# A spectral filter and an MLP on one core: the 24-point Fourier stages on parts of the TensorE array, the filter held in fp32, and results in pairs of PSUM banks

## The chip, the cores and the metric

The kernel runs on one core of a Trainium2 chip. The metric is the device time of one execution in microseconds (us); lower is better. The core has five engines that run side by side, each working through its own instructions in order: TensorE (PE, matrix multiplication; its weight loads are listed as PEld), VectorE (DVE), ScalarE (ACT), GpSimd (POOL) and SyncE (SP). TensorE writes its results into PSUM, a memory of eight banks, each of which holds 512 fp32 values in each of 128 partitions. VectorE or ScalarE must read a result out before its bank can be used again. POOL and SP start most of the transfers (DMA). An engine that has to wait holds back everything that stands behind in its own order.

## The reference

```python
def _attn_ref(x, filt_r, filt_i):                 # x: 8 x 3072 x 256
    X = np.fft.rfft(x, axis=1)
    F = (filt_r + 1j * filt_i)[None, :, :]        # 1537 x 256
    Y = X * F
    return np.fft.irfft(Y, n=x.shape[1], axis=1).astype(np.float32)

def _moe_ref(x, w1, w2, w_out):                   # x: 24576 x 256, w1, w2: 256 x 1024
    h1 = x @ w1
    h2 = x @ w2
    g = np.maximum(h1, h2)
    return (g @ w_out).astype(np.float32)         # w_out: 1024 x 256

def reference(**kwargs):
    ...
    attn_out = _attn_ref(**attn_kwargs)
    B, S, D = attn_out.shape
    x = attn_out.reshape(B * S, D)
    return _moe_ref(x=x, **moe_kwargs)
```

Each of eight sequences is Fourier-transformed along its 3072 positions, multiplied by a filter for each frequency and channel, and transformed back. The result goes, position by position, through two products with a maximum between them, and a third product.

## The kernel before

A transform of 3072 points is done in two stages, since 3072 is 128 x 24. For each batch b there are these pieces:

- **load_x** (POOL's queue): x in six parts, cast to bf16, with 128 positions on the partitions and 24 x 256 values behind them.
- **f1**: the 128-point stage, a matmul with C1 (pa, 512 columns), copied to `at` by ScalarE and written by SP's queue to `ad` in DRAM. **f1_read** reads it back as `bt` in another order, so that the 24 points (real and imaginary) lie on partitions.
- **gen_f2**: sixteen groups g of two frequencies each. A matmul with U (px, 96 x 256 per frequency) is the 24-point stage (called s2 in what follows). VectorE multiplies px by the real and imaginary filter at once into pq (line 384: 1024 results per partition). Two matmuls, with VP and VQ, are the way back (pz, called s3); ScalarE copies pz to `zt`, which SP writes to `zd`. **z_read** fetches `zr` from it in two halves.
- **s4**: for a tile of 512 positions, eight matmuls with G1 (128 columns each) are the 128-point stage back. They go in two halves `dc` of four into a bank each; ScalarE copies the first half and VectorE the second, into y.
- **moe_h(tt, j)** and **moe_o(tt, j)**: the MLP on tile tt in eight steps j. Since max(a, b) = b + relu(a - b), moe_h multiplies y by Wd (w1 - w2) into ph (two matmuls of 512 columns), and a relu makes g. moe_o multiplies y by M (w2 times w_out) and g by Wo into po, and VectorE copies po to `ot`, which POOL's queue writes out.

All results of TensorE but po share six single banks (`ps`); po has two. The instructions of each engine stand in the order in which the program names them (manual_schedule). A main loop runs over 48 tiles, six to a batch, eight steps each, so 48 steps to a batch. In each step come moe_h(tt, j), then moe_o(tt - 1, j), then the pieces that a table `todo` has for this step (load_x, f1 and f2 of later batches), and behind j = 4 mostly s4 of the next tile. Steps are written by hand, such as

```python
plan_f2(b, list(range(0, 34, 2)), 19, 36)
plan_f1(b, b + 2, range(1, 25, 2), 28)
plan_x(b, b + 3, range(5, 48, 4))
```

for b from 3. Before the loop stands the setup: tables of sines (table_c, tables_u, tables_pe), the filter F in bf16 on 96 partitions (loaded in parts, spread by the matmuls of copy_f and by DMA), batch 0's f1 and f2, the MLP's weights, and a few matmuls without use (spin) that keep TensorE going. In batch 0's f2 four of the sixteen products are POOL's.

Of the kernel before, what the change touches and what calls it, by code (L numbers as in the profile page):

```python
# [13 lines left out]
B = 8  # L14
# [3 lines left out]
N1 = 128  # L18
N2 = 24
T = 32  # L20
QP = 96
J = 12
TWO_PI = 6.283184
RND = 12582912.0


@with_exitstack
def kernel(
# [10 lines left out]

    nc = tc.nc
    V, S, G, TE = nc.vector, nc.scalar, nc.gpsimd, nc.tensor

    const = ctx.enter_context(tc.tile_pool(name="const", bufs=1))
    C1 = const.tile([128, 128], BF16)
    G1 = const.tile([128, 128], BF16)
    U = const.tile([QP, T, 2, 48], BF16)  # L60
    VP = const.tile([QP, T, QP], BF16)
    VQ = const.tile([QP, T, QP], BF16)
    F = const.tile([QP, 2, T, D], BF16)
    Wd = const.tile([128, 2, HID], BF16)
    Wo = const.tile([128, 8, D], BF16)
    M = const.tile([128, 2, D], BF16)
    I128 = const.tile([128, 128], BF16)
# [3 lines left out]
    apool = ctx.enter_context(tc.tile_pool(name="apool", bufs=6))  # L71
    bpool = ctx.enter_context(tc.tile_pool(name="bpool", bufs=2))
    pqpool = ctx.enter_context(tc.tile_pool(name="pqpool", bufs=4))
    zpool = ctx.enter_context(tc.tile_pool(name="zpool", bufs=3))
    ps = ctx.enter_context(tc.tile_pool(name="ps", bufs=6, space=bass.MemoryType.PSUM))
    pso = ctx.enter_context(tc.tile_pool(name="pso", bufs=2, space=bass.MemoryType.PSUM))
    zrpool = ctx.enter_context(tc.tile_pool(name="zrpool", bufs=2))
    setup = ExitStack()
    init = setup.enter_context(tc.tile_pool(name="init", bufs=1))
    ctx.enter_context(tc.manual_schedule())  # L80

# [8 lines left out]


    def fsrc(f, row0, dm, nm, dt, nt):
        return bass.AP(f.tensor, f.offset + row0 * D, [[dm * D, nm], [dt * D, nt], [1, D]])

    def load_f(t0, t1):
        for ri, f in enumerate((filt_r, filt_i)):
            for dr in range(2):
                row0, dt = (t0, 1) if dr == 0 else (64 - t0, -1)
                G.dma_start(out=F[24 * dr:24 * dr + 24, ri, t0:t1], in_=fsrc(f, row0, 64, 24, dt, t1 - t0))


    def copy_f(t0, t1, ri, engine):
        for t in range(t0, t1, 2):
            n = min(2, t1 - t)
            pf = ps.tile([QP, 2, D], FP32, tag="ps", name="pf")
            TE.matmul(pf[:, 0:n], DM, F[0:48, ri, t:t + n], start=True, stop=True)  # L106
            if engine is V:
                V.tensor_copy(F[:, ri, t:t + n], pf[:, 0:n])
            else:
                S.activation(F[:, ri, t:t + n], pf[:, 0:n], AF.Copy)  # L110


    F0 = init.tile([QP, 2, D], FP32)

    def load_f0():
        for ri, f in enumerate((filt_r, filt_i)):
            for dr in range(2):
                src = bass.AP(f.tensor, f.offset + 32 * dr * D, [[128 * D, J], [(96 - 64 * dr) * D, 2], [1, D]])
                nc.sync.dma_start(out=F0[24 * dr:24 * dr + 24, ri], in_=src)

    def copy_f0():
        nc.sync.dma_start(out=F0[49:96], in_=F0[1:48])
        nc.sync.dma_start(out=F0[48:49, 1], in_=filt_i[1536:1537, :])
        nc.sync.dma_start(out=F0[48:49, 0], in_=filt_r[1536:1537, :])

    DM = init.tile([48, QP], BF16)
    SW = init.tile([QP, QP], BF16)
    e0 = init.tile([QP, 2], FP32)
    zero = init.tile([128, 1], FP32)
    V.memset(zero, 0.0)  # L130
    pid = init.tile([128, 1], FP32)
    G.iota(pid, pattern=[[1, 1]], base=0, channel_multiplier=1,
           allow_small_or_imprecise_dtypes=True)
    kc = init.tile([128, 2, 2, T], FP32)
    G.iota(kc[:, :, 0], pattern=[[0, 2], [1, T]], base=0, channel_multiplier=0,
           allow_small_or_imprecise_dtypes=True)
    G.iota(kc[:, :, 1], pattern=[[0, 2], [-1, T]], base=64, channel_multiplier=0,
           allow_small_or_imprecise_dtypes=True)
    for c in range(6):
        load_x(0, c)  # L140
    tt_ = init.tile([QP, T], FP32)
    G.iota(tt_, pattern=[[1, T]], base=0, channel_multiplier=0, allow_small_or_imprecise_dtypes=True)

    kb = init.tile([QP, 2, J, 2], FP32)
    k0 = init.tile([QP, 2, J, 2], FP32)
    G.iota(kb, pattern=[[64, 2], [128, J], [64, 2]], base=0, channel_multiplier=0,
           allow_small_or_imprecise_dtypes=True)
    G.iota(k0[:, 0], pattern=[[128, J], [96, 2]], base=0, channel_multiplier=0,
           allow_small_or_imprecise_dtypes=True)
    G.iota(k0[:, 1], pattern=[[128, J], [32, 2]], base=32, channel_multiplier=0,  # L150
           allow_small_or_imprecise_dtypes=True)
    V.memset(DM, 0.0)
    V.memset(I128, 0.0)
    V.memset(SW, 0.0)
    for b0 in (0, 48):
        G.affine_select(out=DM, in_=DM, pattern=[[-1, QP]], compare_op=OP.not_equal,
                        fill=1.0, base=b0, channel_multiplier=1)
    G.affine_select(out=I128, in_=I128, pattern=[[-1, 128]], compare_op=OP.not_equal,
# [99 lines left out]
    def tables_pe():  # L258
# [9 lines left out]
        for t in list(range(2, T, 5)) + [0]:  # L268
# [7 lines left out]
            if len(todo) > 2:  # L276
                swap(*todo.pop(0))
# [314 lines left out]
```

## Time and profile before

| | us |
|---|---|
| three runs | 592.22, 586.09, 596.46 |
| median | 592.22 |
| span of the profiled execution | 584.8 |
| TensorE busy, matmuls | 543.8 (93%) |
| TensorE busy, weight loads | 399.7 (68%) |
| VectorE busy | 327.6 (56%) |
| ScalarE busy | 338.8 (58%) |
| POOL busy | 77.2 (13%) |
| mean granted TensorE clock | 0.970 |

The profiled execution's own time is not on its page beside the span; the fastest of the runs is 1.3 us longer than that span. A matmul's busy time holds its way through the array, which overlaps with the next matmul. So the time that one costs in a row of them is the distance between their starts. The costliest groups are po's matmuls (line 443, 231.3 us), relu on ScalarE (line 423, 177.1) and the products with the filter (line 384, 150.9). The first output leaves at 89.6 us, the last at 580.5.

### The profile page before, as it was taken

To read this page: it belongs to the slowest core of one execution; us is meant where nothing else is said; L and a number is where in the kernel's file an instruction comes from. 1 tells how busy PE (TensorE), PEld (TensorE's weight loads), DVE (VectorE), ACT (ScalarE), POOL (GpSimd) and SP (SyncE) were. 2 spreads that over 40 slices of the span, in tenths; PEclk is the share of its full clock that TensorE was granted. 3 is DMA by queue.
4 is the path that set the end of the run, shared out by engine and by line. 5 is a ranking of instruction groups with operands and counts; after the bars stand their busy time and mean duration, and the time that the engine had idled before them with its cause. 6 is when DMAs were issued, how large, how long until landed. Compare 5 with 4: busy or idle time off the path is not lost.

```text
span 584.8 us, 9932 instructions
## 1 busy us (share of the span) xinstructions
PE 543.8 (93%) x3981; PEld 399.7 (68%) x4050; DVE 327.6 (56%) x423; ACT 338.8 (58%) x608; POOL 77.2 (13%) x131
## 2 busy tenths in 40 slices
PE   4687797999999999997999999999999999999996
PEld 0456554776678667775777777776777777777774
DVE  8845132773368437753567466654765477734342
ACT  5744383565766766763676566655675455554541
POOL 6034510110020011111110002000000000000000
PEclk9985898899999999999999999999999999999999
DMA  8987588575397778989477946894457524241112
GB/s 165 218 149 228 132 195 180 131 180 157 138 229 161 199 211 183 228 203 239 133 174 204 214 115 166 199 215 127 131 155 176 154 100 118 93 124 73 73 59 86
DMA packets 76642, 93.81 MB, mean 160 GB/s; under 512 B 4627, under 2 KB 56389, under 8 KB 75524
## 3 DMA queue, kind: packets, MB, share of 16 engines
q1 hardware_dynamic: 59492, 53.37, 35.7%
q0 software_dynamic: 17104, 39.81, 27.4%
q8 instruction: 31, 0.51, 0.3%
q14 instruction: 15, 0.12, 0.1%
HBM read 56.63 MB, written 50.33 MB: 183 GB/s over the span
## 4 chain that ended last, share of the span: by engine, by line
PE 44%; issue 33%; DMA 16%; POOL 3%; DVE 2%; ACT 1%; POOLq 0%; SPq 0%; DVEq 0%; ACTq 0%
PE po L443 14%; PE ph L418 12%; DMA bt<-ad 6%; PE po L438 3%; PE pz L365 3%; PE pz L366 3%; PE pa L336 3%; PE px L375 3%; DMA xb<-in_x_dram 2%; DMA zr<-zd 2%; DMA ad<-at 2%; PE py L402 2%; POOL out_dram L449 2%; DVE pqt L384 2%; DMA zd<-zt 2%
## 5 line engine op out<-in xcount | busy, mean ns | idle before, releaser
L423 ACT ACTIVATE gt<-ph 128x512 bf16<-128x512 f32 x298 | 177.1, 594 | 102.2 <-PE ph L418 92.8
L443 PE MATMUL po<-Wo,gt 128*128 128x256 bf16 x1536 | 231.3, 274 | 2.4 <-issue 0.2
L384 DVE TENSOR_TENSOR pqt<-px,F 96x1024 bf16<-96x1024 f32 x124 | 150.9, 1219 | 86.8 <-PE px L375 77.8
L443 PEld LDWEIGHTS <-gt 128*128 128x128 bf16 x1536 | 150.7, 98 | 59.0 <-issue 0.8
L367 ACT ACTIVATE zt<-pz 96x512 bf16<-96x512 f32 x128 | 75.6, 592 | 86.0 <-PE pz L366 66.3
L445 DVE COPY ot<-po 128x512 f32<-128x512 f32 x96 | 66.4, 692 | 92.8 <-PE po L443 92.8
L449 POOL DMA_DIRECT2D out_dram<-ot x48 | 25.8, 537 | 461.4 <-DVE ot L445 451.4
L418 PEld LDWEIGHTS <-Wd 128*128 128x128 bf16 x768 | 73.9, 99 | 18.5 <-issue 3.2
L421 DVE TENSOR_SCALAR gt<-ph 128x512 bf16<-128x512 f32 x86 | 58.8, 684 | 32.5 <-PE ph L418 32.0
L337 ACT ACTIVATE at<-pa 128x512 bf16<-128x512 f32 x96 | 56.8, 599 | 30.6 <-PE pa L336 26.7
L365 PE MATMUL pz<-pqt,VP 96*96 96x256 bf16 x256 | 67.8, 289 | 5.7 <-POOL pqt L384 3.7
L366 PE MATMUL pz<-pqt,VQ 96*96 96x256 bf16 x256 | 67.8, 289 | 0.0
L375 PE MATMUL px<-bt,U 96*96 96x256 bf16 x256 | 52.7, 291 | 8.0 <-DMA bt<-ad 8.0
L336 PE MATMUL pa<-xb,C_58 128*128 128x512 bf16 x96 | 38.3, 411 | 8.3 <-DMA xb<-in_x_dram 8.2
L375 PEld LDWEIGHTS <-U 96*96 96x96 bf16 x256 | 32.7, 134 | 10.6 <-issue 4.7
L366 PEld LDWEIGHTS <-VQ 96*96 96x96 bf16 x256 | 33.5, 131 | 6.5 <-issue 6.2
L365 PEld LDWEIGHTS <-VP 96*96 96x96 bf16 x256 | 33.6, 131 | 3.2 <-DVE pqt L384 2.6
L402 PE MATMUL py<-G_59,zr 128*128 128x128 bf16 x384 | 29.3, 219 | 2.8 <-DMA zr<-zd 2.8
L402 PEld LDWEIGHTS <-zr 128*128 128x128 bf16 x384 | 25.3, 98 | 5.3 <-issue 3.8
L88 POOL DMA_DIRECT2D xb<-in_x_dram x48 | 26.1, 563 | 0.4 <-issue 0.3
L336 PEld LDWEIGHTS <-C_58 128*128 128x128 bf16 x96 | 9.4, 101 | 14.4 <-DMA xb<-in_x_dram 5.3
L106 PE MATMUL pf<-F,DM 48*96 48x512 bf16 x16 | 7.4, 628 | 5.2 <-DMA F<-in_filt_r_dram 4.9
(325 smaller groups left out, 496.9 us busy)
## 6 DMA issues: line engine op xcount, KB each, us to landing
out_dram<-ot POOLq DMA_DIRECT2D x48, 512.0 KB, 3.5
xb<-in_x_dram POOLq DMA_DIRECT2D x48, 256.0 KB, 6.7
ad<-at SPq DMA_DIRECT2D x48, 256.0 KB, 2.6
bt<-ad SPq DMA_DIRECT2D x16, 768.0 KB, 6.8
zd<-zt SPq DMA_DIRECT2D x64, 192.0 KB, 3.4
zr<-zd SPq DMA_DIRECT2D x16, 768.0 KB, 6.8
w1f<-in_moe_w_dram SPq DMA_DIRECT2D x1, 1024.0 KB
w2f<-in_moe_w_dram SPq DMA_DIRECT2D x1, 1024.0 KB
```

What stands on the lines that cost most here:

```text
L336: TE.matmul(pa, C1, xb[b, c // 2][:, 2 * (c % 2):2 * (c % 2) + 2], start=True, stop=True)
L365: TE.matmul(pz[:, i], VP[:, 2 * g + i], pqt[:, 0, i], start=True, stop=False)
L366: TE.matmul(pz[:, i], VQ[:, 2 * g + i], pqt[:, 1, i], start=False, stop=True)
L367: S.activation(zt[:, 2 * (g % 2):2 * (g % 2) + 2], pz, AF.Copy)
L375: TE.matmul(px[:, i], U[:, 2 * g + i].rearrange("p a b -> p (a b)"), bt_[:, 2 * g + i], start=True, stop=True)
L384: E.tensor_tensor(pqt, px.rearrange("p (o i) d -> p o i d", o=1).to_broadcast([QP, 2, 2, D]), F[:, :, 2 * g:2 * g + 2], OP.mult)
L402: TE.matmul(py[:, n], zr[b][:, 4 * i + n, 128 * dc:128 * dc + 128], G1, start=True, stop=True)
L418: TE.matmul(ph, Wd[:, dc, 128 * j:128 * j + 128], y_[:, dc].rearrange("p a b -> p (a b)"), start=(dc == 0), stop=(dc == 1))
L421: V.tensor_scalar(gt[tt][:, j], ph, 0.0, None, OP.max)
L423: S.activation(gt[tt][:, j], ph, AF.Relu)
L443: TE.matmul(p_, g_[:, jj, 128 * n:128 * n + 128], Wo[:, jj], start=False, stop=(jj == 7))
L445: V.tensor_copy(ot[tt][:, n - 1:n + 1], po[tt])
```

## The change

- **24-point stages on parts of the array.** s2's U is laid out so that one matmul uses 64 rows (48 filled) and 32 columns of the array, and s3's VT so that one uses 32 rows (24 filled) and 64 columns. An s2 is 16 matmuls of 256 columns for each s (of eight), over four column places q and two row places dr. An s3 is 64 for each v (a pair of s). Each has its own weight load.
- **Filter in fp32.** F lies once in fp32, in blocks of 32 partitions, loaded by 29 DMAs of POOL's queue over a zeroed tile. Copies by matmul and DMA fall away; one extra row fN is multiplied by itself.
- **Pairs of banks.** pa, px, pz and py are tiles of two banks (`pair`), from a pool of two in the main loop (four in the setup); ph gets two banks of its own. Copies of pa and pz take 1024 elements at once. Both halves of s4 lie in one pair.
- **Who copies.** A small count of busy time (`clock`, `pick`) decides, while the program is written, whether ScalarE or VectorE takes a relu or copy. s4's halves stay with ScalarE and VectorE.
- **Steps.** s2, product and s3 get steps of their own. zd is written in 16 parts a batch instead of 8, zr read in three instead of two. In the setup all products of batch 0 are VectorE's, and w1 and w2 are asked for earlier.

The core of the diff:

```diff
-    ps = ctx.enter_context(tc.tile_pool(name="ps", bufs=6, space=bass.MemoryType.PSUM))
...
+    def pair(name):
+        return pp.tile([128, 2, 512], FP32, tag="pp", name=name)
...
+    def s2(b, v):
+        for s in (2 * v, 2 * v + 1):
+            px = pair("px")
+            for ri in range(2):
+                for q in range(4):
+                    for dr in range(2):
+                        o = ((8 * q + s) * 2 + ri) * 24
+                        TE.matmul(px[32 * q:32 * q + 32, dr, D * ri:D * ri + D], U[64 * dr:64 * dr + 48, o:o + 32],
+                                  bt[b][64 * dr:64 * dr + 48, 8 * q + s], start=True, stop=True)
+            pe(320)
+            px_[b, s] = px
+
+    def mul(b, s):
+        px = px_.pop((b, s))
+        pq = pqpool.tile([128, 2, 2, 512], BF16, tag="pq", name="pq")
+        for i in range(2):
+            V.tensor_tensor(pq[0:120, i].rearrange("p a (r d) -> p a r d", r=2),
+                            px[0:120].rearrange("p a (r d) -> p a r d", r=2),
+                            F[0:120, i, :, s].rearrange("p a (o d) -> p a o d", o=1).to_broadcast([120, 2, 2, D]),
+                            OP.mult)
+            if i == 0 and s == 0:
+                V.tensor_tensor(pq[0:1, 0, 0, D:2 * D], px[0:1, 0, D:2 * D], fN, OP.mult)
...
+    def s3(b, v, force=None):
+        pz = [pair("pz") for _ in range(2)]
+        for si in range(2):
+            s = 2 * v + si
+            pq = pq_.pop((b, s))
+            for n, (o, i, ri) in enumerate(((0, 0, 0), (2, 1, 1), (1, 0, 1), (1, 1, 0))):
+                for q in range(4):
+                    for dr in range(2):
+                        a = ((s * 2 + dr) * 3 + o) * 48
+                        TE.matmul(pz[q // 2][64 * dr:64 * dr + 64, q % 2, D * si:D * si + D],
+                                  VT[32 * q:32 * q + 24, a:a + 64],
+                                  pq[32 * q:32 * q + 24, i, dr, D * ri:D * ri + D], start=(n == 0), stop=(n == 3))
+        pe(1070)
...
     def s4(tt):
...
+        py = pair("py")
         for dc in range(2):
-            py = ps.tile([128, 4, 128], FP32, tag="ps")
             for n in range(4):
-                TE.matmul(py[:, n], zr[b][:, 4 * i + n, 128 * dc:128 * dc + 128], G1,
+                TE.matmul(py[:, dc, 128 * n:128 * n + 128], zr[b][:, 4 * i + n, 128 * dc:128 * dc + 128], G1,
                           start=True, stop=True)
...
+            copy(y_[:, dc].rearrange("p a b -> p (a b)"), py[:, dc], 512, scale=1.0 / 1536.0, force=("act", "dve")[dc])
...
-        ph = ps.tile([128, 512], FP32, tag="ps")
+        ph = psh.tile([128, 512], FP32, tag="ph", name="ph")
...
+    pp = ctx.enter_context(tc.tile_pool(name="pp", bufs=2, space=bass.MemoryType.PSUM))
+    psh = ctx.enter_context(tc.tile_pool(name="psh", bufs=2, space=bass.MemoryType.PSUM))
+    pso = ctx.enter_context(tc.tile_pool(name="pso", bufs=2, space=bass.MemoryType.PSUM))
...
+    def plan_f2(b, steps, gap, read):
+        for v, n in enumerate(steps):
+            n += 48 * b
+            plan(0, n, s2, b, v)
+            plan(0, n, mul, b, 2 * v)
+            plan(0, n + 2, mul, b, 2 * v + 1)
+            plan(0, n + gap, s3, b, v)
+        plan(0, 48 * b + read, z_read, b)
...
+    plan_f1(1, -45, 1, -39)
+    plan_f2(1, (-27, -22, -17, -12), 5, -6)
+    plan_x(2, -86, 2)
+    plan_f1(2, -59, 2, -48)
+    plan_f2(2, (-38, -32, -26, -19), 6, -11)
     for b in range(3, B):
...
+        plan_x(b, -98, 3)
+        plan_f1(b, -76, 2, -64)
+        plan_f2(b, (-52, -42, -31, -21), 6, -13)
...
+            for fn, a in todo.pop(8 * tt + j, ()):
                 fn(*a)
-            if j == (4 if i < 5 else 6 if b else 7) and tt + 1 < 6 * B:
+            if j == 4 and tt + 1 < 6 * B:
                 s4(tt + 1)
```

Steps below zero count back from the first step of batch b. So s2 of batch b stands in steps 44, 6, 17 and 27 of the 48 that belong to earlier batches, f1 in every second step from 20 to 30, and s4 behind the pieces of steps 4, 12, 20, 28, 36 and 44.

## The prediction

> **What bounds the kernel now.** I read the page's busy shares first, then busy time by stage, then one tile in the timeline. By stage, each row gives the stretch, its length, then busy time of PE, PEld, DVE, ACT and POOL, the granted clock, DMA share and GB/s:
>
> ```profile
> 0.00:72.00 72.00, 50.56 (x231) 32.28 (x232) 40.76 (x82) 36.34 (x67) 29.62 (x43) 0.86 0.81 180
> ...
> 72.00:152.10 80.10, 74.11 (x521) 52.26 (x530) 38.26 (x45) 49.37 (x91) 8.56 (x17) 0.94 0.68 162
> ...
> 217.00:289.00 72.00, 67.43 (x508) 50.24 (x516) 43.51 (x50) 42.19 (x78) 10.21 (x20) 0.98 0.82 197
> ...
> 351.70:415.20 63.50, 62.42 (x486) 47.14 (x494) 39.05 (x46) 39.07 (x71) 5.88 (x12) 1.00 0.67 170
> ...
> 535.20:584.80 49.60, 43.92 (x339) 32.22 (x343) 17.61 (x26) 19.81 (x34) 3.73 (x7) 0.99 0.19 75
> ```
>
> Setup and batch 0's transform take 72 us. After that the core is a TensorE stream: 62.42 of 63.50 us in a full batch, with VectorE and ScalarE at 39 each. So a microsecond taken off TensorE counts there, and a microsecond for which TensorE is made to wait counts too. Only the batches from 72 to 152 and from 217 to 289 us hold slack. Inside a tile:
>
> ```profile
> 405.28 0.59 PE L418 MATMUL ph<-y__4791,Wd 128*128 128x512 bf16 x2
> ...
> 406.25 0.38 PE L375 MATMUL px<-bt,U 96*96 96x256 bf16 x2
> ...
> 406.48 0.27 PE L365 MATMUL pz<-pqt,VP 96*96 96x256 bf16 x1
> ...
> 406.58 0.27 PE L366 MATMUL pz<-pqt,VQ 96*96 96x256 bf16 x1
> ...
> 406.67 1.22 DVE L384 TENSOR_TENSOR pqt<-px,F 96x1024 bf16<-96x1024 f32 x1 [0.57 <-PE px L375]
> 406.69 0.27 PE L365 MATMUL pz<-pqt,VP 96*96 96x256 bf16 x1
> ...
> 409.74 0.61 PE L402 MATMUL py<-G_59,zr 128*128 128x128 bf16 x8
> ...
> 410.43 0.58 ACT L405 ACTIVATE y__4904<-py 128x512 bf16<-128x512 f32 x1
> 410.64 0.68 DVE L407 TENSOR_SCALAR y__4904<-py 128x512 bf16<-128x512 f32 x1
> ```
>
> Starts 0.11 us apart are the cost of a 256-column matmul; its listed 0.27 holds about 0.16 more of latency, under the next ones. The eight of L402 follow at 0.056 us without a break, though two engines read their results: each half of py is a tile of its own.
>
> **Work from 72 us on.** One step (moe_h and moe_o) is 2 x 0.215 + 5 x 0.109 = 0.975 us. A tile is eight steps and s4 (0.43), 8.23; the last outputs stand 8.27 apart. 48 tiles make 397, seven f1 at 12 x 0.215 make 18, seven f2 at 96 x 0.109 = 10.46 make 73. That is 488 of the 512.8 us to the end; about 4 are the tail, some 20 waits.
>
> **Removed and halved: the 24-point stages.** s2 becomes 16 matmuls of 256 columns per s on eight tiles, s3 64 per v. The trace has no matmul on a part of the array. If eight stream side by side, an s2 is two waves, 0.213, an s3 eight, 0.853: 8 x 0.213 + 4 x 0.853 = 5.1 us per batch. If each load and matmul pair went out only as fast as the closest pairs of this trace, 0.056 (L402), it is 384 x 0.056 = 21.5. Rows of 256 columns are set by streaming, not by issue, so I stay near the first end and add one to two waves for filling and mode changes: 0.32 and 1.07, or 6.84 us per batch. Against 10.46 that saves 3.62 x 7 = **25 us** (bounds: 37 saved, 77 lost).
>
> [...]
>
> **Added (1): s4 waits for its own reader.** Both halves of py now lie in one pair of banks. In the built order the fifth matmul of every s4 waits for ScalarE's copy of the first half, and VectorE's copy waits for it as well. The first half ends 3 x 0.056 + 0.219 = 0.387 us after its start; ScalarE starts 0.03 later, takes 0.594 (row of 512 elements), and 0.05 more passes until TensorE starts (after a VectorE end at 38.45 a weight load starts at 38.50). The second half starts at 1.06, not 0.224: 0.84 us, in every tile, on the bounding engine. Queued behind are moe_h of the next step and so all later work. 48 x 0.84 = **40 us**. Bounds: 0.2 per tile if ScalarE's end is seen early (10 us), 1.1 if it is behind with another copy (53).
>
> **Added (2): two pairs for f1, s2, s3 and s4.** Six single banks served all of them and ph; now ph has two banks and the four others share two pairs. An s2 takes both pairs, and each is held until two multiplications (1.22 each, row L384: still 1024 elements) have read it. A wide copy of 1024 elements I take at 1.01 on ScalarE, from 0.28 for 128 and 0.594 for 512 (bounds 0.6 and 1.2). From the end of streaming to a reader's start: 0.2. Counting in steps of a batch from the fourth on, with the waits of the built order:
>
> - Step 44: s2, then s4, which waits for the first pair: 0.2 + 2.44 + 0.35 (the extra row fN) + 0.05, less 0.32 of the second s2: 2.7.
> - Step 12: s3, then s4, which waits for a wide copy: 0.2 + 1.01 + 0.05 = 1.25.
> - Step 20: s4 waits for the second multiplication of the s2 at 17: 5.13 after its first half; TensorE is there at 0.32 + 3 x 0.975 + 0.43 = 3.68: 1.45.
> - Steps 23 and 24: s3 after f1, f1 after s3, one step (0.975) apart where 1.26 is needed: 0.6 together.
> - Step 28: f1 waits for the multiplication of the s2 at 27, 2.69 less 1.3: 1.4; then s4 for f1's copy: 1.25.
>
> Together 8.65 for each of batches 3 to 6. Batch 7 has no f1 beside it: 5.35. Batch 2 (s3 and s2 in one step, f1 behind them) comes to 9 in the same way, batch 1 to 12, of which some 4 are for x and for zr, read only two steps ahead. 34.6 + 5.35 + 9 + 12 = **61 us**. Bounds: three quarters and five quarters of it.
>
> **Hidden.** Fewer, wider copies and F in fp32 leave VectorE's 1.22 as it is; both engines stay near 40 of 60 us per batch. Without that cover a late relu would hold ph, with two banks 1.5 us later. The 16 instead of 8 writes of zd per batch go out on SP, which has nothing else due; their landing (3.4 us) and zr's (6.8) fit the nine steps before s4, except in batch 1. Were they late, s4 would wait by the difference.
>
> **Setup.** The bound is DMA (share 0.81) and then multiplication: the last bt lands at about 30 us, the first product starts at 37.23, the last at 55.65 on POOL, and s4 starts at 70.7. Afterwards 29 loads of F leave POOL's queue, 0.6 each, behind six of x: the last at 25, landing (8 to 11 in the rows) at 33 to 36. SP's queue brings w forward, into the same DMA engines. All 16 products are VectorE's: 16 x 1.22 from about 36 ends at 56, then s3, two wide copies on ScalarE (4), zd (2.5 to 3.4) and the first piece of zr (3): 66. **4 us** gained (0 to 8).
>
> **Sum.** 488 - 25 + 40 + 61 + 4 = 568 against 512.8, less 4 in setup: +52. On the span, 584.8 + 52 = 637. The page shows no other time of this execution; the fastest of three runs is 586.09, the median 592.22, and on that it is **644 us**.
>
> **The rivals.**
> 1. Tiles don't overlap: weight loads or issue take turns, as in the pairs of 0.056. For it: four times the instructions, each with a load. Against: nothing here is bound by issue. 644 + 7 x (21.5 - 6.84) = 747; at half that pace (0.028, 10.8 per batch) 671. It decides from about 0.02 per pair. Chance 0.17.
> 2. The s4 wait isn't there in time, since half a pair is released as soon as needed: 644 - 40 = 604, at the 2% bound. Against it stands the built order. Chance 0.11.
> 3. Faster: the pairs come free before TensorE asks. While it waits in s4, VectorE (39 of 63 us busy) gets on with its products, so the 61 are the same time counted twice. The place is the s4 and f1 behind each s2. 644 - 61 = 583; with the tiles at 5.1 per batch, 571. It decides once less than a tenth of the 61 is left and the tiles stream. Against: the product is emitted behind the s2 that it reads, so TensorE's wait cannot come first. Chance 0.08.
>
> A smaller risk sits in the forecast: around step 44 TensorE waits 2.7 and then 0.84 us, nearly without work. The row from 72 to 152 us shows a clock of 0.94 with 6 us idle; such a loss would add up to 5 us per batch.
>
> **How the numbers follow.** The forecast has 0.64. Its own range, from the bounds of the waits (25 less, 25 more) and of the tiles, is 612 to 675. To hold 8 in 10 it reaches down to rival 2 and up towards half of rival 1: 606 to 700. 2% is about what a measurement of this kernel can tell from no change: faster 0.08 (rival 3), same 0.10 (most of rival 2), slower 0.82.
>
> **What would show it.** Right: TensorE's busy share falls below 90%; py's copies on VectorE start 0.6 us or more after ScalarE's end; the waits of s4 and f1 name the products; tiles of the last batch stand 9.1 us apart, not 8.27; s3 lasts about 1.1 us. Wrong: last tiles 8.3 apart (no s4 wait), s3 of 3 us (rival 1), a full batch under 62 us (rival 3).

## The result, and the profile after

| | before | after |
|---|---|---|
| median of the runs, us | 592.8 | 743.35 |
| lowest, highest run, us | 586.09, 596.46 | 735.09, 749.21 |
| span of the profiled execution, us | 584.8 | 741.1 |
| mean granted TensorE clock | 0.970 | 0.881 |
| TensorE busy, matmuls | 543.8 (93%) | 562.2 (76%) |
| first s4 starts at, us | 70.7 | 89.1 |

The changed kernel takes 1.256 times as long (95% interval 1.243 to 1.268). The forecast of slower was right; its 644 us, and the end of its range at 700, were not.

The stretches by stage of the changed kernel, with the columns as in the prediction's rows (length, busy time of PE, PEld, DVE, ACT and POOL, clock, DMA share, GB/s):

```profile
0.00:88.00 88.00, 37.94 (x601) 19.10 (x602) 34.62 (x75) 25.51 (x24) 32.30 (x60) 0.73 0.85 156
...
370.70:455.30 84.60, 68.16 (x782) 43.94 (x780) 37.36 (x41) 40.33 (x64) 6.44 (x12) 0.88 0.57 132
...
687.90:741.10 53.20, 44.92 (x346) 32.39 (x343) 9.18 (x14) 27.20 (x46) 3.68 (x7) 0.98 0.18 70
```

A full batch takes 84.6 us where 62 to 64 were needed. TensorE is idle for 16.4 of them, and it is also busy for longer than before (68.16 us, not 62.42) although its 24-point stages are shorter (8 x 0.28 and 4 x 1.01 are 6.28 us, not 10.46): the clock is 0.88, not 1.00. What it waits for stands behind the bar in the page's groups (busy time, mean ns of one, then idle time just before and what ended most of it):

```profile
L384 PE MATMUL py<-G,zr 128*128 128x128 bf16 x384 | 41.6, 238 | 82.2 <-ACT yt L93 35.1
L326 PE MATMUL px<-bt,U 48*32 48x256 bf16 x1024 | 25.7, 299 | 56.0 <-DMA bt<-ad 46.9
L354 PE MATMUL pz<-pq,VT 24*64 24x256 bf16 x2048 | 39.3, 289 | 5.3 <-DVE pq L335 5.3
```

The first row's 35.1 us are the wait inside s4 that the prediction had. The second row's 46.9 us it had not: bt is late. One batch in TensorE's timeline (start, length, what; in brackets the idle time before it and its releaser):

```profile
374.58 1.08 PE L354 MATMUL pz<-pq,VT 24*64 24x256 bf16 x64
376.77 0.38 PE L384 MATMUL py<-G,zr 128*128 128x128 bf16 x4 [1.11 <-ACT zt L93]
377.84 0.58 PE L384 MATMUL py<-G,zr 128*128 128x128 bf16 x4 [0.69 <-ACT yt L93]
378.22 1.06 PE L397 MATMUL ph<-yt,Wd 128*128 128x512 bf16 x2
...
384.59 0.63 PE L326 MATMUL px<-bt,U 48*32 48x256 bf16 x32
...
389.74 0.40 PE L384 MATMUL py<-G,zr 128*128 128x128 bf16 x4 [1.06 <-DVE pq L335]
390.83 0.38 PE L384 MATMUL py<-G,zr 128*128 128x128 bf16 x4 [0.69 <-ACT yt L93]
391.05 0.59 PE L397 MATMUL ph<-yt,Wd 128*128 128x512 bf16 x2
...
403.60 0.60 PE L304 MATMUL pa<-xb,C 128*128 128x512 bf16 x2 [1.18 <-DVE pq L335]
405.37 0.59 PE L384 MATMUL py<-G,zr 128*128 128x128 bf16 x4 [1.16 <-ACT at L93]
...
430.63 0.63 PE L326 MATMUL px<-bt,U 48*32 48x256 bf16 x31 [2.43 <-DMA bt<-ad]
436.65 0.61 PE L384 MATMUL py<-G,zr 128*128 128x128 bf16 x4 [5.39 <-DMA zr<-zd]
437.94 0.58 PE L384 MATMUL py<-G,zr 128*128 128x128 bf16 x4 [0.69 <-ACT yt L93]
438.31 1.06 PE L397 MATMUL ph<-yt,Wd 128*128 128x512 bf16 x2
```

Three things are to be seen. The 24-point stages are fast: 64 matmuls of s3 in 1.01 us, two s2 of 16 in 0.56. The waits for pairs are where the prediction put them, about 1.1 us each. And there are two long waits that end with a DMA, 2.43 and 5.39 us, after which two matmuls of 512 columns last 1.06 us together in place of 0.59: TensorE comes back at half clock (0.50 granted from 436.65 to 442.40 us).

Why zr is late, from the chain of work in order of time (start, length, what), and the transfers of the two kernels (KB each, median us from issue to landing), first of after, then of before:

```profile
421.25 0.82 SPq L367
...
423.76 9.90 DMA zd<-zt
...
433.74 2.86 DMA zr<-zd
```

```profile
bt<-ad SPq DMA_DIRECT2D x16, 768.0 KB, 14.0
zd<-zt SPq DMA_DIRECT2D x128, 96.0 KB, 2.7
zr<-zd SPq DMA_DIRECT2D x16, 640.0 KB, 5.1
```

```profile
bt<-ad SPq DMA_DIRECT2D x16, 768.0 KB, 6.8
zd<-zt SPq DMA_DIRECT2D x64, 192.0 KB, 3.4
zr<-zd SPq DMA_DIRECT2D x16, 768.0 KB, 6.8
```

bt has the same bytes in the same number of transfers and lands after 14.0 us, not 6.8. The last four writes of zd stand right behind it in SP's queue, so one of them lands after 9.90 us. The median of 2.7 over all 128 hides that.

### The profile page after: what moved, and what is told of

Its sections match the earlier page's. It is cut to its first block, busy times and chain, and to the rows that moved or that the text cites. A ratio compares the mean times of both kernels' runs of the same rounds, so it can differ in the third digit from the quotient of the medians.

```text
span 741.1 us, 14786 instructions
## 1 busy us (share of the span) xinstructions
PE 562.2 (76%) x6449; PEld 360.9 (49%) x6449; DVE 301.5 (41%) x364; ACT 344.4 (46%) x528; POOL 78.9 (11%) x147
## 4 chain that ended last, share of the span: by engine, by line
PE 43%; DMA 21%; issue 18%; ACT 7%; DVE 7%; SPq 2%; POOL 1%; POOLq 0%; ACTq 0%; DVEq 0%
PE ph L397 14%; PE po L420 13%; DMA zd<-zt 7%; DVE pq L335 6%; PE py L384 4%; DMA bt<-ad 4%; PE pz L354 4%; PE po L415 3%; DMA Wo<-in_moe_w_out_dram 3%; ACT yt L93 3%; DMA F<-in_filt_r_dram 3%; DMA zr<-zd 2%; PE pa L304 2%; ACT zt L93 2%; SPq L367 2%
## 5 line engine op out<-in xcount | busy, mean ns | idle before, releaser
L397 PE MATMUL ph<-yt,Wd 128*128 128x512 bf16 x768 | 247.0, 405 | 1.1 <-DVE yt L97 0.6
L335 DVE TENSOR_TENSOR pq<-px,F 120x1024 bf16<-120x1024 f32 x128 | 149.0, 1213 | 55.0 <-PE px L326 55.0
L384 PE MATMUL py<-G,zr 128*128 128x128 bf16 x384 | 41.6, 238 | 82.2 <-ACT yt L93 35.1
L415 PE MATMUL po<-M,yt 128*128 128x256 bf16 x384 | 77.1, 284 | 0.0
L93 ACT ACTIVATE zt<-pz 112x1024 bf16<-112x1024 f32 x36 | 36.4, 1022 | 71.1 <-PE pz L354 68.6
L326 PE MATMUL px<-bt,U 48*32 48x256 bf16 x1024 | 25.7, 299 | 56.0 <-DMA bt<-ad 46.9
L415 PEld LDWEIGHTS <-yt 128*128 128x128 bf16 x384 | 39.4, 103 | 50.2 <-issue 10.1
L93 ACT ACTIVATE at<-pa 128x1024 bf16<-128x1024 f32 x40 | 40.7, 1023 | 39.7 <-PE pa L304 32.2
L93 ACT ACTIVATE ot<-po 128x512 f32<-128x512 f32 x83 | 49.6, 597 | 8.0 <-PE po L420 5.0
L304 PE MATMUL pa<-xb,C 128*128 128x512 bf16 x96 | 35.2, 454 | 19.1 <-DMA xb<-in_x_dram 8.1
L354 PE MATMUL pz<-pq,VT 24*64 24x256 bf16 x2048 | 39.3, 289 | 5.3 <-DVE pq L335 5.3
```

The lines of the kernel that those rows point to most:

```text
L93: S.activation(dst, src, AF.Copy, scale=1.0 if scale is None else scale)
L304: TE.matmul(pa[:, i], C1, xb[b, c][:, 2 * i:2 * i + 2].rearrange("p a b -> p (a b)"), start=True, stop=True)
L326: TE.matmul(px[32 * q:32 * q + 32, dr, D * ri:D * ri + D], U[64 * dr:64 * dr + 48, o:o + 32], bt[b][64 * dr:64 * dr + 48, 8 * q + s], star ...
L335: V.tensor_tensor(pq[0:120, i].rearrange("p a (r d) -> p a r d", r=2), px[0:120].rearrange("p a (r d) -> p a r d", r=2), F[0:120, i, :, s] ...
L354: TE.matmul(pz[q // 2][64 * dr:64 * dr + 64, q % 2, D * si:D * si + D], VT[32 * q:32 * q + 24, a:a + 64], pq[32 * q:32 * q + 24, i, dr, D ...
L384: TE.matmul(py[:, dc, 128 * n:128 * n + 128], zr[b][:, 4 * i + n, 128 * dc:128 * dc + 128], G1, start=True, stop=True)
```

## The experiments

Times are medians; a ratio is to the kernel before, run on the same chip, with its 95% interval.

### The wait inside s4

```diff
             pe(220)
+        for dc in range(2):
             copy(y_[:, dc].rearrange("p a b -> p (a b)"), py[:, dc], 512, ...
```

> The kernel after with one edit: s4 issues its eight matmuls first and then the two copies, so that the fifth matmul no longer waits for ScalarE. If the wait costs what the forecast put for it, 0.84 us in each of 48 tiles, 743 becomes 703 us, and the outputs of the last batch come 8.3 us apart instead of 9.1. If each long stop around an s4 also costs clock (177.8 us at half clock in the kernel after, 37.3 before), a few microseconds more go: 690 to 700. Rival: the wait only moves, because the pair that s4 uses must be free again for the next user anyway; then the last outputs stay 9.1 apart and the time above 730.

Measured: 701.44 us, ratio 1.191 (1.181 to 1.200), 42 us less than 743.35. Outputs of the last batch, POOL's timeline, first after, then this kernel:

```profile
706.08 0.53 POOL L427 DMA_DIRECT2D out_dram<-ot  x1 [8.58 <-ACT ot L93]
715.19 0.53 POOL L427 DMA_DIRECT2D out_dram<-ot  x1 [8.58 <-ACT ot L93]
```

```profile
666.46 0.53 POOL L428 DMA_DIRECT2D out_dram<-ot  x1 [7.74 <-ACT ot L93]
674.73 0.53 POOL L428 DMA_DIRECT2D out_dram<-ot  x1 [7.74 <-ACT ot L93]
```

They come 9.11 us apart there and 8.27 here: 0.84 in each tile, to the hundredth what the forecast had. The wait didn't move elsewhere.

### Why bt is late

Before, one read of bt writes 96 partitions, at 40 to 46 ns for a packet of 512 bytes. After, each read writes 48: 0 to 47, or 64 to 111, at 67 to 89 ns. The first theory, of the halves in what follows, was a guess of mine that no trace had shown: a read into one half of the partitions alone (0 to 63, or 64 and up) is slower for that reason.

```diff
-        for dr in range(2):
-            SP.dma_start(out=bt[b][64 * dr:64 * dr + 48], in_=src[dr])
+        for t in range(0, T, 4):
+            for dr in range(2):
+                SP.dma_start(out=bt[b][64 * dr:64 * dr + 48, t:t + 4], in_=src[dr][:, t:t + 4])
```

> The kernel after with bt read by 16 DMAs in place of 2: four t at a time, the two halves of the partitions in turn, all on SP's queue. [...] With both halves in flight together the last piece lands about 8 us after the first was issued instead of 14, the waits for bt and for the first zr around step 44 (2.4 and 5.4 us in the batch from 370.7 us) go or shrink below 3 together, and with them some of the half clock: 690 to 715 us in place of 743. Rival: the landing is late because of the load of x, outputs and zd beside it, or because of the queue's order alone. Then packets stay near 80 ns, bt lands after 13 us or more, and the time stays within 1% of 743.

Measured: 722.85 us, ratio 1.223 (1.207 to 1.239). The 512-byte packets took 27 ns in the median, and some 330 to 435 of them came in a us, so the halves taken in turn are fast. The issues now set that rate: SP names a read of 192 packets every 0.49 us, some 395 packets in a us. It needs 8 to 10 us for the 16 reads, and zd stands behind them: the wait for zr at step 44 is still 6.35 us. The gain is 20 us, less than the 28 to 53 that were expected.

```diff
+            E = S if dr and b else SP
-            SP.dma_start(out=bt[b][64 * dr:64 * dr + 48], in_=src[dr])
+            E.dma_start(out=bt[b][64 * dr:64 * dr + 48], in_=src[dr])
```

> The kernel after with the second half of bt (partitions 64 to 111) read from ScalarE's DMA queue, from batch 1 on, the first half still from SP's. Theory of the halves: two queues bring packets of both halves at once, so landing falls from 14 to 8 or 9 us, as with pieces in turn; ScalarE holds the issue until the last ad has landed, up to 2 us in each batch, which may delay a few relus: 695 to 720 us. Rival, that two transfers from two queues only take turns and each packet stays near 80 ns: landing stays at 13 to 15 us, and with ScalarE's wait the time is 743 to 755.

Measured: 717.56 us, ratio 1.218 (1.208 to 1.229). Landing hardly fell (12 to 13 us). The halves are issued at 400.74 and 400.76 us, but most of the second one's packets come only 4 to 5 us after the first one's, which run nearly alone at 78 to 87 ns until then; where both run together, a packet takes 40 to 80 ns. zd now stands behind half of bt, and the wait for zr there fell to 3.07 us. The time is in the range; the landing that was expected is not.

The same question, put to the kernel before:

```diff
-        for h in (1, 0):
-            src = ...[:, 16 * h:16 * h + 16]
-            nc.sync.dma_start(out=bt[b][:, 16 * h:16 * h + 16], in_=src)
+        for lo, hi in ((0, 64), (64, 96)):
+            nc.sync.dma_start(out=bt[b][lo:hi], in_=src[lo:hi])
```

> The kernel before with its bt read in two DMAs of partitions 0 to 63 and 64 to 95 with all t, in place of two of all 96 partitions with half of the t each. Theory of the halves: packets of 512 bytes go from 27 to 45 ns up to about 80 ns, and bt lands after 11 to 14 us instead of 6.8. The bt of this kernel is asked for some 20 steps ahead of its use and zd's writes behind it have time, so the time hardly moves: 592 to 600 us. Rival, that load and not the choice of partitions makes the landing late: it stays at 6 to 8 us.

Measured: 615.26 us, ratio 1.044 (1.033 to 1.055). Here the first theory fell: the packets took 41 to 52 ns, some 400 in a us, though each read wrote to one half. (The time grew for another reason: no t is complete before the second read has landed, and TensorE waited 28.6 us for bt in the whole run, where it had waited 8.0.) So half of the partitions is not the cause. The next run cuts at 48 instead:

> The kernel before with bt read in two DMAs of partitions 0 to 47 and 48 to 95. With the cut at 64 the packets stayed at 42 to 49 ns, as uncut, so it is not enough that a DMA writes to one half of the partitions. [...] Rival: 48 partitions or the source's stride is what is slow: then both DMAs are at 80 ns. Second rival: neither is slow, and the slow reads of the kernel after come from what runs beside them: both at 42 to 50 ns. Time: 610 to 625 us (the first t are complete only when the second DMA has landed, as with the cut at 64: 615).

```diff
-        for lo, hi in ((0, 64), (64, 96)):
+        for lo, hi in ((0, 48), (48, 96)):
```

Measured: 623.83 us (one run). Both reads are of 48 partitions, from the same kind of source, and one is slow and the other is not; neither of the two rivals came out. The rates, counted from the trace's packet records in stretches of 1 us inside the reads of bt, in full batches:

```
read writes partitions    kernel      packets in a us   ns of one
0-95                      before      405-465           40-46
0-63, then 64-95          b_bt64      365-437           41-52
0-47 and 64-111           after       211-289           67-89
0-47                      b_bt48      209-291           66-92
48-95                     b_bt48      375-430           44-51
0-31 and 64-95            a_bt32      340-402           47-55
32-47 and 96-111          a_bt32      194-260           75-98
```

The number of partitions alone doesn't sort these rates either: 48 of them ran at 209 to 291 packets in a us from 0 and at 375 to 430 from 48, and a read of 64 was nearly as fast as one of 96 (365 to 437 against 405 to 465). The records name no engine of a packet, so what makes a read slow is not shown.

```diff
+        for lo, hi in ((0, 32), (32, 48)):
             for dr in range(2):
-                SP.dma_start(out=bt[b][64 * dr:64 * dr + 48], in_=src[dr])
+                SP.dma_start(out=bt[b][64 * dr + lo:64 * dr + hi], in_=src[dr][lo:hi])
```

> The kernel after with each half of bt read in two DMAs, by partitions: 0 to 31 and 64 to 95 first, then 32 to 47 and 96 to 111. [...] Time 730 to 742 us. Rival: any DMA on fewer than 64 partitions runs near 80 ns and 250 in a us; then all four look alike and the time stays at 743 or above.

Measured: 719.74 us (one run), better than the 730 to 742 expected, with the rates of the table: cutting 48 into 32 and 16 makes one part faster, leaves one slow, and all of it lands sooner (the parts after 7.7 and 10.1 us in the median, where the reads of 48 took 14.0). In these runs it mattered how the halves were cut and ordered, by 20 to 26 us (722.85, 717.56 and 719.74 against 743.35).

### Why zr is late

```diff
-                SP.dma_start(out=dst, in_=zt[64 * dr:64 * dr + 48, :, si])
+                (G if v == 3 and b > 2 else SP).dma_start(out=dst, in_=zt[...])
...
-            SP.dma_start(out=zr[b][:, lo:hi], in_=src[:, lo:hi])
+            (G if b > 2 else SP).dma_start(out=zr[b][:, lo:hi], in_=src[:, lo:hi])
```

> The kernel after with the last four zd writes and the three zr reads of each batch from 3 on issued on POOL's queue instead of SP's, where they stand right behind bt's two reads. Theory of the queue: those writes are late (9.9 us) only because they stand behind bt's slow packets. Then the wait for zr near step 44 (5.4 us in the batch from 370.7 us) falls below 1.5, the wait for bt (2.4) stays or grows by 1, and with the half clock that goes with it the time is 700 to 722 us. Rival: the packets of both share the same 16 DMA engines, so that another queue gains little: zr wait above 4 us, time above 733.

Measured: 734.47 us, ratio 1.240 (1.211 to 1.269), 9 us less than after, with overlapping intervals: the time is the rival's, the wait lies between the two. The wait for zr fell from 5.39 to 2.64 us in that batch and was 4.00 in the next, but the writes still needed a median of 11.5 us on POOL's queue. So the queue's order is only a part of it; what the rest is, is not shown.

### The half clock

```diff
+    def fill(n):
+        ph = psh.tile([128, 512], FP32, tag="ph", name="ph")
+        for i in range(n):
+            TE.matmul(ph, C1, U[:, 0:512], start=True, stop=True)
...
+        plan(0, 48 * b - 52, fill, 10)
         plan_f2(b, (-52, -42, -31, -21), 6, -13)
+        plan(0, 48 * b - 52, fill, 20)
```

> The kernel after with 30 matmuls of 512 columns added in each batch from 3 on, that nobody reads: 10 ahead of the s2 at step 44 (2.2 us at full clock) and 20 between that s2 and its s4 (4.3 us), where TensorE waits for bt and zr (2.4 and 5.4 us). Nothing is left out. Theory of the clock: after the long waits TensorE streams at half clock for some 3 to 4 us, and the waits' idle time is what brings that about. With the fill the waits that are left are short, the half clock after step 44 goes, and the time falls by 2 to 4 us per batch although work was added: 722 to 735 us, with a mean clock above 0.89. Rival: the half clock does not come from these waits; then the fill is hidden at best: 741 to 755 us with the clock as before.

Measured: 726.6 us, ratio 1.227 (1.189 to 1.264): 17 us less for 30 more matmuls in each of five batches (two runs, of 723.26 and 729.93 us; its interval still overlaps that of after, 1.243 to 1.268, so the trace is the better evidence). The row by stage and TensorE's timeline of this kernel:

```profile
368.30:446.90 78.60, 68.94 (x801) 44.54 (x810) 37.32 (x41) 40.30 (x64) 6.41 (x12) 0.98 0.61 142
```

```profile
422.76 2.32 PE L487 MATMUL ph<-U,C 128*128 128x512 bf16 x10
...
425.69 0.63 PE L326 MATMUL px<-bt,U 48*32 48x256 bf16 x31 [0.40 <-DMA bt<-ad]
426.25 4.49 PE L487 MATMUL ph<-U,C 128*128 128x512 bf16 x19
430.65 0.40 PE L384 MATMUL py<-G,zr 128*128 128x128 bf16 x4
...
431.95 0.59 PE L397 MATMUL ph<-yt,Wd 128*128 128x512 bf16 x2
```

The filling work takes the place of the waits, the two matmuls behind them last 0.59 us again, the clock of this batch is 0.98, and it takes 78.6 us instead of 84.6. That is the best of four full batches: the clock is 0.94 to 0.98 in them, where it was 0.88 to 0.90, and each is 0.7 to 6.0 us shorter, 13 together. So the half clock after step 44 comes from TensorE's idle time there. In after it stands behind the 2.43 and 5.39 us. But half clock also follows the 1.11 and 0.69 around s4 at 376.77 (the two matmuls at 378.22 take 1.06, the granted clock is 0.50), while after the 1.06 and 0.69 around 389.74 the two at 391.05 take 0.59 (at 1.00). So in this trace less idle time can be enough, but nearly the same waits do not always bring half clock; what decides it is not shown.

### The setup

In the changed kernel F was in at 49.8 us (a memset of VectorE's waited for it), and the matmuls on the rest of bt started at 55.8. The first product followed at 56.5, where it had started at 37.23:

```profile
49.77 0.27 DVE L128 MEMSET F<- 1x256 f32 x1 [21.40 <-DMA F<-in_filt_i_dram]
```

```profile
55.79 1.91 PE L326 MATMUL px<-bt,U 48*32 48x256 bf16 x63 [8.25 <-DMA bt<-ad]
```

Four runs; in none does s4(0) come back to 70.7 us.

```diff
-    apool = ctx.enter_context(tc.tile_pool(name="apool", bufs=4))
+    apool = ctx.enter_context(tc.tile_pool(name="apool", bufs=6))
...
-    load_w(SP)
...
         s3(0, v, "act")
+        if v == 0:
+            load_w(SP)
+    prep_wd()
```

> The kernel after with two parts of its setup undone: six buffers for f1's results instead of four, and w1 and w2 asked for only behind the first writes of zd, instead of right behind bt. prep_wd then comes after the products. Theory: w's 2 MB and the late ad writes hold up bt (25 us landing, first px at 55.8 us). Then bt lands in 12 to 17 us, the first px is at 45 to 49, s4(0) at 78 to 83 instead of 89.1, and the time is 733 to 738. Rival: the 29 loads of F (3.1 MB on POOL's queue) set it; then the first px stays after 53 us and s4(0) within 2 us of 89.

Measured: 735.39 us, ratio 1.242 (1.210 to 1.274); s4(0) at 89.4. The first product still starts at 55.1. w is not the cause.

```diff
-    load_f(G, 1)
...
     f1_read(0)
+    G.tensor_copy(hold0, bt[0][0:1, 0:1, 0:1])
+    load_f(G, 1)
```

> The kernel after with six buffers for f1's results, w1 and w2 behind the first writes of zd, and the imaginary half of F (14 loads) held on POOL until bt has landed. With the first two edits alone s4(0) stayed at 89.4 us and the time at 735. Theory: F's loads take the DMA engines from ad and bt (bt issued at 29.5 us, landed at 54). Now ad and bt land 8 to 14 us earlier, the imaginary half of F lands at 45 to 52, the first product starts at 46 to 52 instead of 55 to 56 and s4(0) at 80 to 86. Time 724 to 733. Rival: F itself is what is late; held back it lands later still, and s4(0) is at 90 to 98, the time 737 to 750.

Measured: 742.81 us, ratio 1.257 (1.240 to 1.273). The rival came out. bt was complete at 43 us, 12 us earlier, but then F was what came last. VectorE's timeline of this kernel:

```profile
56.95 0.27 DVE L128 MEMSET F<- 1x256 f32 x1 [29.11 <-DMA F<-in_filt_i_dram]
...
57.60 1.23 DVE L335 TENSOR_TENSOR pq<-px,F 120x1024 bf16<-120x1024 f32 x1 [0.23 <-issue]
```

```diff
-    load_f(G, 0)
-    load_f(G, 1)
+    for ri in range(2):
+        load_f(G, ri, (0, 1))
...
+    for ri in range(2):
+        load_f(S, ri, (2, 3))
```

> The kernel after with the loads of F dealt to two queues: the blocks of partitions 0 to 63 on POOL's, those of 64 to 127 on ScalarE's, behind its copies of f1; with six buffers for f1's results, and w1 and w2 behind the first writes of zd. [...] From two queues, for two halves of the partitions, F is in at 28 to 38 us, the first product starts at 40 to 48 instead of 56, and s4(0) at 72 to 81 instead of 89: 723 to 734 us. Rival: all the setup's transfers together fill the DMA engines (share 0.85), whatever their order: then s4(0) stays at 85 to 91.

Measured: 754.23 us, ratio 1.279 (1.267 to 1.291). This run doesn't decide the question, whether loads in a row to the same few partitions are slow: ScalarE issued its 12 loads between 12.9 and 53.5 us and did no other work for 39.0 us of that, the sine table of U came at 53.5, and s4(0) at 99.3.

```diff
+        for qs in ((0, 2), (1, 3)):
+            for part in range(3):
+                for q in qs:
...
-        for q in range(4):
...
-            for dr in range(2):
```

> The kernel after with the 24 large loads of F in another order on the same queue, blocks 0 and 2 and then 1 and 3 in turn, so that loads next to each other write other partitions (0 to 11, 64 to 75, 12 to 23, 76 to 87), and six buffers for f1's results. In the run before, half of the loads on ScalarE's queue held ScalarE itself until 53 us, so it did not test the theory that loads in a row which write the same few partitions are slow (packets of 4 KB took 290 to 650 ns). With it, F is in at 36 to 44 us instead of 49.8, the first product starts at 46 to 52 instead of 56.5 and s4(0) at 80 to 86 instead of 89.1: time 735 to 741. Rival: the transfers together are what is slow; then F is in at 47 to 52, s4(0) at 87 to 92.

Measured: 740.18 us (one run). F was in at 50.5 us, the first product at 56.9, s4(0) at 89.5: the order of F's loads isn't it either. What the runs show: with F's loads on POOL's queue, bt of batch 0 and F together need until 54 to 57 us, whichever comes first, and all transfers together move 120 to 128 GB/s between 40 and 50 us. F's packets of 8 KB took a median of 0.91 us in the last run, a tenth of them 0.31 or less. Why they are slow is not shown.

### All causes together

```diff
+        for t in range(0, T, 8):
             for dr in range(2):
-                SP.dma_start(out=bt[b][64 * dr:64 * dr + 48], in_=src[dr])
+                SP.dma_start(out=bt[b][64 * dr:64 * dr + 48, t:t + 8], in_=src[dr][:, t:t + 8])
...
+        for dc in range(2):
             copy(y_[:, dc].rearrange("p a b -> p (a b)"), py[:, dc], 512, ...
```

> The kernel after with two edits: s4's copies behind its eight matmuls, and bt read by eight DMAs, eight t at a time, the two halves in turn. Alone the first gave 701 us; 16 pieces of bt gave 723 (20 less than after), with SP busy for 8 us issuing them and zr 6.4 us late behind it. If the two are separate causes, their gains add up, and fewer issues shorten zr's wait by 2 to 4 us per batch: 672 to 686 us. Rival: both feed the same wait for zr near step 44; then 690 to 701.

Measured: 669 us, from two runs of 663.8 and 674.2. Against 701 for the copies alone that is 27 to 38 us, where 16 pieces of bt alone had brought 20: the two gains at least add up.

```diff
-    def s2(b, v):
-        for s in (2 * v, 2 * v + 1):
+    def s2(b, *ss):
+        for s in ss:
...
+        ((-91, -88, -83, -80, -77, -75), -73, (-60, -59, -51, -46, -41, -26, -24, -21), (-54, -38, -18, -16), -15),
...
+            if j == 4 and tt + 1 < 6 * B:
+                s4(tt + 1)
             for fn, a in todo.pop(8 * tt + j, ()):
                 fn(*a)
```

The added row holds the steps of a batch from the fourth on: f1, f1_read, the eight s2, the four s3, z_read.

> The kernel with s4's copies last and bt in eight pieces, and with other steps: each s2 of one s by itself, so that it takes one pair of banks and not both, s4 ahead of the pieces of its step, and s2, s3 and f1 at steps chosen so that a pair is asked for about when it should be free again (an s2 holds one for 3.4 us, f1 for 1.8, s4 for 1.5, s3 both for 2.6); bt is asked for at least 12 steps ahead of its first use and zr 15 steps ahead. Theory: the time of the kernel after is work (463 us from s4(0) on), plus waits that come from these steps, plus half clock that comes from the waits. Then some 20 to 40 us of waits remain, and with s4(0) at 89: 572 to 605 us. Rival: tiled matmuls or pairs of banks cost something of their own that no order takes away; then over 640 us.

Measured: 600.15 us, ratio 1.016 (1.009 to 1.023). Its rows by stage:

```profile
86.00:189.30 103.30, 78.95 (x855) 48.39 (x866) 42.62 (x49) 50.97 (x78) 11.31 (x22) 0.90 0.72 169
...
252.10:312.40 60.30, 59.67 (x770) 40.27 (x781) 37.27 (x41) 39.84 (x63) 6.43 (x12) 1.00 0.72 184
```

A full batch takes 60.30 us, with TensorE busy for 59.67 and the clock at 1.00. It is the same work as in the 84.60 us of after, with the same tiles, pairs of banks and fp32 filter. So the 24 us of a full batch come from the order of the work and from how bt's reads are cut, not from the tiles, the pairs or the filter: 0.6 of 16.4 us of waiting are left, and 8.5 us of busy time (68.16 less 59.67) are gone, most of them the half clock. Which of this run's edits brings how much isn't told apart, but for the copies and the pieces of bt above.

What it still loses to the kernel before lies ahead of batch 2. Four runs went after that.

```diff
+        load_f(S, ri, (2, 3))
     f1_read(0)
+    G.tensor_copy(hold, bt[0][64:65, T - 1:T, 0:1])
+    for c in range(6):
+        load_x(1, c)
...
```

> The kernel with the other steps (600 us, ratio 1.016 to before), with F's loads on two queues and w later as in the run above, and batch 1's x asked for as soon as bt of batch 0 has landed, instead of after the first zr. Full batches stood 60.3 us apart there (before: 62 to 64), so what it lost to before lies ahead of batch 2: s4(0) at 86 (before 70.7) and batch 0's stretch of 101 us. If the setup shrinks as expected and f1 of batch 1 no longer waits for x (4 us): 578 to 590 us, ratio 0.975 to 0.995. Rival: what batch 0 loses is one chain from f1 of batch 1 to its zr; then only the setup's gain counts, and if that is not there, 595 to 600.

```diff
-        ((-70, -67, -62, -59, -55, -54), -53, (-44, -41, -36, -33, -30, -28, -20, -18), (-38, -25, -23, -14), -13),
+        ((-70, -64, -61, -59, -56, -55), -54, (-46, -42, -36, -34, -31, -28, -21, -18), (-39, -25, -23, -15), -9),
...
```

The rows of the other batches change as well; the row shown is batch 2's.

> As the run above, with another list of steps, found with SP's queue taken as one that waits in order: batch 2's f1 and bt start a step or six apart from before, so that bt's eight pieces do not stand behind zr of batch 1. Two waits of batch 1 (6.7 for zr, 7.4 for bt of batch 2) should shrink by 4 to 8 together: 572 to 586 us. Rival: the chain of batch 1 is what it is; then within 3 us of the run above.

Measured: 607.9 us (ratio 1.031, 1.026 to 1.036) and 611.87 (1.038, 1.031 to 1.046). Both take over the setup of the run with two queues, and s4(0) is at 92.3 and 88.9, against 86.2 without. With f1 no longer waiting for x, the stretch from s4(0) to the end of the span is 513 us in the first, against 511 without: the early x brought nothing.

```diff
-    spin(24)
+    spin(8)
...
-        (...), -53, (-44, -41, -36, -33, -30, -28, -20, -18), (-38, -25, -23, -14), -13),
+        (...), -53, (-39, -36, -34, -33, -30, -28, -23, -22), (-31, -25, -17, -15), -12),
```

> The kernel with the other steps (600 us, ratio 1.016) with two edits: batch 2's s2 begin five steps later and its s3 are spread to match, because its bt, asked for behind zr of batch 1 on SP's queue, kept TensorE waiting for 7 us and at half clock behind that; and the 24 warming matmuls that stand ahead of s4(0) are 8 (4 us less, as zr had landed 3.6 us before they ended). Expected: the wait for bt of batch 2 goes (7 us, and 3 to 5 of half clock), s4(0) at 83: 584 to 592 us. Rival: later s2 collide with what stands there, and the time stays at 597 to 603.

Measured: 602.84 us (1.020, 1.014 to 1.026). s4(0) is at 81.2, 5 us earlier than in the run with 600 us, from the shorter warming row. But what batch 0 won, batch 1 gave back: 92.5 and 75.8 us, against 103.1 and 62.8. The rival that was named for this run came out.

```diff
+        for qs in ((0, 2), (1, 3)):
```

> As the run above, and the loads of F in turn as in the first run of this set. If that order brings s4(0) 4 to 8 us forward: 577 to 588 us, faster than before by about 1%; else the same as the run above.

Measured: 601.93 us (1.019, 1.014 to 1.025), the same within the intervals. No version here beats the kernel before.

## Why the prediction was right or wrong

**Removed (the 24-point stages): right.** An s3 takes 1.01 us against the 1.07 forecast, an s2 0.28 against 0.32. With the waits gone, a full batch stands at 60.3 us against 62 to 64 before, where 3.62 less was forecast. Rival 1 gives 747 us, close to the result by luck, and is wrong all the same: the tiles overlap, 16 ns for a pair of load and matmul in s3. The one to two waves added for filling and mode changes were an estimate that no run shows by itself: an s3 took 1.01 us where eight waves make 0.853.

**Added (1), the wait inside s4: right** to 0.84 us a tile, 40 forecast, 42 measured by taking it out.

**Added (2), the waits for pairs: right in place, a little too large.** 1.11, 1.06, 1.18 and 1.16 us were forecast as 1.25, 1.45, 1.4 and 1.25; of the 0.6 of steps 23 and 24 hardly anything is there. At step 44 the wait for a pair does not show, since zr is later still.

**Hidden: this step failed.** It took bt's landing as unchanged and the writes of zd as covered by nine steps. bt's reads were the same bytes from the same queue, but in reads of 48 partitions from 0 and from 64, and 14.0 us instead of 6.8 leave nothing of that cover. The step said what late transfers would cost, the difference, but gave no price for their being late. In the batch from 370.7 us the two waits are 7.8 us, 5 more than the 2.7 that the sum had there, and half clock stands behind them.

**The smaller risk, the clock: mis-sized.** It stood outside the sum, with up to 5 us for a batch. In full batches TensorE was busy 8.5 us longer for the same work (68.16 less 59.67). Most of it is the clock: a row of 84.6 us at 0.88 has some 20 us at half clock, of which some 6 are waits, so I estimate 7 us. The rest, 1.5 us, is not taken apart.

**Setup: wrong in sign.** Forecast 4 us less, measured 18 more. The step counted products, copies and landings one after the other and let F land at 33 to 36 us with bt at about 30. F was in at 49.8, the matmuls on the rest of bt started at 55.8, and the first product at 56.5, 20 us later than the step had it. Four runs did not settle which limit F and bt meet; 3.6 us are the warming matmuls, which here end after zr has landed.

**The sum.** Forecast and measured spans are 637 and 741, 104 apart. Setup is 22 of that (4 less against 18 more). In the four batches from 285.2 to 622.7 us it is 11.6 each, 46 in all: they take 84.4 us on average, and the forecast's terms make 72.8 (62.7 before, less 3.62, plus 6 x 0.84 for s4, plus 8.65 for the pairs). The 11.6 are about 8.5 for the longer busy time, 5.1 for bt and zr at step 44, less 1.4 for the smaller waits for pairs and less 0.6 for the faster tiles. So in these four batches the clock, with some 30 us, weighs more than the late transfers themselves, with 20. The remaining 36 lie in the other batches and are not taken apart here; waits for bt and zr of 3.89, 5.45, 1.65 and 3.50 us are among them. The sum also dropped, without a reason, the some 20 us of waits that it had counted in the kernel before.

**The signs.** TensorE's busy share fell below 90% (76%), the last tiles stood 9.11 us apart and an s3 took 1.01 us, as named for being right, and yet the time was 100 us off: none of the signs was for the transfers or the clock.

## What to carry to other kernels

When a layout changes, price each transfer again by the partitions that it now writes, not by its bytes: the same 768 KB took twice as long in reads of 48 partitions from 0 and from 64, and what stood behind it in the queue was late with it. Waits of a few microseconds in a TensorE stream can cost more than themselves (behind 5.39 us the clock here was 0.50 for another 5.75), so put them into the sum with the clock behind them, or fill them. And a bad time can be the order and not the change: the same tiles and banks gave 743 and 600 us, though 600 is still not under the 592 of before.

## What the runs showed of the hardware

- A read of 48 partitions from 0 ran at 209 to 291 packets of 512 bytes in a us, one of 48 partitions from 48 at 375 to 430, in the same kernel (b_bt48).
- 64 matmuls of 24 rows and 64 columns with 256 columns to stream, each with its own load, took 1.01 us: 16 ns each.
- Work that nobody reads, put into the waits (a_fill), made four full batches 13 us shorter together and took their clock from 0.88 to 0.90 up to 0.94 to 0.98.
- DMAs issued from ScalarE held ScalarE: 12 loads, named ahead of the sine table, kept it until 53.5 us (a_setup3).
